# Moving the rounding of weights and one block's sums in the head of a convolution and MLP kernel

## The chip, the cores and the metric

The kernel runs on one core of one Trainium2 chip. The metric is the device time of one execution in microseconds (us); for the kernel before, three runs are given with their median. Engines are named as the profile names them: PE is TensorE (matmuls; PEld its weight loads), DVE is VectorE, ACT is ScalarE, POOL is GpSimd, SP is SyncE, which here only issues transfers. A "q" behind an engine's name is its queue of issued transfers (DMA).

## The reference

The input x = q has 2048 rows of 448 values. Each row is normalized (xn), and the output is the sum of x and two branches:

```python
xn = _layernorm(x, axis=-1)
return x + _A_ref(xn, A_k, A_v, A_shift_k, A_ssm_k, A_ssm_D) + _B_ref(xn, B_w1, B_b1, B_w2)
```

Branch A is a state-space convolution: k goes through a causal convolution of four taps and is multiplied by v (kv); kv is convolved with ssm_k per channel over all 2048 steps by Fourier transforms of length 4096; kv times ssm_D is added; the result is multiplied by xn. Branch B is a two-layer perceptron: h = xn w1 + b1 (1792 columns), act = h tanh(softplus(h)) (Mish), and act w2 (448 columns).

## The kernel before

**The perceptron.** The rows are cut into 8 chunks of 256 (CH), the 1792 hidden columns into 7 pairs of 128-column blocks (NP). One step takes one chunk and one pair: g1_mm (line 474) multiplies xn by w1, mish (line 497) applies bias and Mish on ACT, g2_mm (line 509) multiplies by w2 two steps later (G2_LAG). To keep precision each operand is a high part, rounded to the fp32r type, and a low part, the rest: XH and XL of xn, w1h and w1l, w2h and w2l, ach and acl of the activation. The high part is a copy on ACT, the low part a subtraction on DVE (split, line 79; w1_hi and w1_lo, lines 348 and 351). Each product is three matmuls: high by high, high by low, low by high. In the first chunk g1_mm takes them pair by pair as high weights by XH, high by XL, low weights by XH, and then the remainder of 64 rows (the fourth block of w1h, whose upper half holds its own low part, line 354), first for one block of 128 columns, then for the other; the very first pair has an order of its own (line 490). Its two blocks have a PSUM tile each, those of later pairs share one.

**The convolution** runs between the perceptron's steps: Fourier transforms written as matmuls in three stages. Of the first stage, the head holds one block of ssm_k: f1_mm (line 124) multiplies it by the constant f1 into two PSUM tiles e and o; f1_fold (line 134) copies o to SBUF on ACT and has DVE write the sum and the difference of e and o (lines 138 and 140); f1_out (line 143) stores them to DRAM. The PSUM pool of these blocks holds two tiles (line 52), so the next block's f1_mm waits until both sums are done.

**What sets the order.** The program is scheduled by hand (line 565). Every step has two slots: an even one, in which g1_mm is issued, and an odd one with mish and g2_mm. The lists plan (function at, line 97) and plan2 (function after, line 100) hold what is issued before and after the body of a slot; each engine works through its instructions in the order of issue and waits by semaphores. Before slot 0 comes the head, lines 643 to 700. There SP loads the first chunk of q, the first piece of w1 in two halves, one block of ssm_k (H_HEAD), the second and third pieces of w1 and the first of w2, in that order; ACT issues the loads of the identity (needed by the transposes of xn) and of f1; POOL issues that of the bias b1t (line 666). Then come the statistics of the two row blocks (DVE), the reciprocal standard deviations (POOL, power, line 398), normalization, transposes on PE, and XH and XL. Before the change the block of the head is folded behind slot 3 (line 699); w1's second piece is rounded in slot 0, its third in slot 2, its fourth in slot 4 (line 598); w2's first piece behind slot 3 (line 600). Raw weights pass through a pool of four buffers (kr, line 112): w1's fourth, w2's second, w1's fifth, w2's third and w1's sixth piece each wait for a buffer, and so for the low part made from what it held.

The tile idr has 256 columns: the identity stands in the first 128, and from chunk 5 on the whole tile is overwritten by rows of mean and deviation (nt_row, line 427).

Of the kernel before, what the change touches and what calls it, by code (L numbers as in the profile page):

```python
# [7 lines left out]
F32 = mybir.dt.float32  # L8
# [6 lines left out]
S, D, F = 2048, 448, 1792  # L15
NJ = 16
NF = F // 128
# [6 lines left out]
G2_LAG = 2  # L24
H_HEAD = 1
# [11 lines left out]


@with_exitstack
def tile_kernel(ctx: ExitStack, tc, q, qT, k, v, sk, hT, sD, w10, w1, b1, w2, c_f1, c_id, c_g, c_gi, c_i2, out):  # L40
    nc = tc.nc
    V = nc.vector

    def pool(name, bufs=1, stack=ctx, **kw):
        return stack.enter_context(tc.tile_pool(name=name, bufs=bufs, **kw))

    cp = pool("consts")
# [11 lines left out]
    E = dp.tile([NJ * 4, 64, D], F32, name="E")  # L59
    MR = {c: dp.tile([2, CH], F32, name="MR") for c in range(NT, NCHUNK)}  # L60

    f1 = cp.tile([128, 64], F32, name="f1")
    idr = cp.tile([128, CH], F32, name="idr")
    ident = idr[:, 0:128]
    mhalf = cp.tile([128, 2], F32, name="mhalf")
    b1t = cp.tile([128, NF], F32, name="b1t")
    mv = cp.tile([128, NJ, 2], F32, name="mv")
# [11 lines left out]
    def split(h, l, raw):  # L79
        nc.scalar.copy(h, raw)  # L80
        V.tensor_sub(l, raw, h)  # L81
# [7 lines left out]
    def dv(n=1):  # L89
        for _ in range(n):  # L90
            if drip:
                drip.pop(0)()


    plan, plan2 = {}, {}

    def at(slot, fn, *args):
        plan.setdefault(int(slot), []).append((fn, args))

    def after(slot, fn, *args):  # L100
        plan2.setdefault(int(slot), []).append((fn, args))
# [10 lines left out]
    def kr():  # L112
        return sp1.tile([128, 4, CH], F32, name="kr", bufs=4)
# [17 lines left out]
                    nc.tensor.matmul(ps[h][64 * jj:64 * jj + 64, b, :D], f1[rg:rg + 32], x[rg:rg + 32, jj],  # L131
                                     start=True, stop=True, tile_position=(rg, 64 * jj))

    def f1_fold(g, key):
        ST[key, g] = st = sp1.tile([128, 2, 2, D], F32, name="st", bufs=2)
        e, o = (p[:, :, :D] for p in PS.pop((key, g)))
        nc.scalar.copy(st[:, 1], o)  # L137
        V.tensor_add(st[:, 0], e, st[:, 1])  # L138
        dv()
        V.tensor_sub(st[:, 1], e, st[:, 1])  # L140
        dv()

    def f1_out(dst, g, key, eng=nc.scalar):
        st = ST.pop((key, g))
# [200 lines left out]
    def w1_raw(p, a, b):  # L345
        return RW["1", p][:, :, a:b] if p else RW["1", 0][:, a // 128]

    def w1_hi(p, a=0, b=256):
        nc.scalar.copy(w1h[:, :, 256 * p + a:256 * p + b], w1_raw(p, a, b))

    def w1_lo(p, a=0, b=256):
        fs, rw = slice(256 * p + a, 256 * p + b), w1_raw(p, a, b)
        V.tensor_sub(w1l[:, :, fs], rw[:, 0:3], w1h[:, 0:3, fs])  # L353
        V.tensor_sub(w1h[64:128, 3, fs], rw[64:128, 3], w1h[64:128, 3, fs])
# [5 lines left out]
    def w2_load(p):  # L360
        RW["2", p] = rw = xt() if p > 4 else kr().rearrange("p a b -> p (a b)")[:, :2 * D].rearrange("p (a b) -> p a b", a=2)
        nc.sync.dma_start(rw, w2[:, 2 * p:2 * p + 2])
# [18 lines left out]
    def ln_parts(c):  # L381
        st = mp.tile([128, 2, 6], F32, name="bst", bufs=2)
        ve = mp.tile([128, 2], F32, name="ve", bufs=2)
        if c < NT:
            XN[c] = xn = xn_tile().rearrange("p a b -> p (a b)").rearrange("p (j d) -> p j d", j=2)
        eng = nc.gpsimd if 0 < c < NCHUNK - 1 else V

        def stats(jj):
            V.bn_stats(st[:, jj], Q[c][:, jj])

        def aggr(jj):
            V.bn_aggr(mv[:, 2 * c + jj], st[:, jj])

        def eps(a, b):
            V.tensor_scalar(ve[:, a:b], mv[:, 2 * c + a:2 * c + b, 1], EPS, None, op0=ALU.add)  # L395

        def power(a, b):
            nc.gpsimd.tensor_tensor(rs(c)[:, a:b], ve[:, a:b], mhalf[:, a:b], op=ALU.pow)  # L398

        def norm(jj):  # L400
            j = 2 * c + jj
            eng.tensor_scalar(xn[:, jj, :D], Q[c][:, jj], mv[:, j, 0:1], rs(c)[:, jj:jj + 1],  # L402
                              op0=ALU.subtract, op1=ALU.mult)

        def tail(a, b, copy=eng.tensor_copy):
            copy(xn[:, a:b, D:], xn[:, a:b, D - 64:D])

        return stats, aggr, eps, power, norm, tail, ve
# [88 lines left out]
    def mish(i):  # L497
        p = pairs[i][1]
        ps = P1.pop(i)
        a = mp.tile([128, 2, CH], F32, name="a", bufs=2)  # L500
        for n in range(2):
            nc.scalar.activation(a[:, n], ps[n], AF.Mish, bias=b1t[:, 2 * p + n:2 * p + n + 1])  # L502
        ah = mp.tile([128, 2, CH], F32R, name="ach", bufs=3)
        al = mp.tile([128, 2, CH], F32R, name="acl", bufs=3)
        split(ah, al, a)
        dv()
        AHL[i] = ah, al
# [60 lines left out]
    for g, t in H_AT.items():  # L568
        if g != H_HEAD:
            at(t - 5 if t > 7 else t - 3, h_load, g)  # L570
        if g == 0:
            after(t - 2, lambda: V.tensor_add(HT[0][0:1, 0], HT[0][0:1, 0], SD.pop()))
        at(t, f1_mm, HT, g, "h")
        if t in POOL_H:
            after(t, taps_pool, *POOL_H[t])
        after(t, f1_fold, g, "h")
        at(t + (2 if t < 12 else 3), f1_out, Dh, g, "h", nc.gpsimd if t < 12 else nc.scalar)
# [4 lines left out]
    for g, t in enumerate(KV_AT):  # L582
        d = t - (KV_AT[g - 1] if g else t - 6)
        at(t - d - (3 if g > 1 else 2), k_load, g)
        at(t - d - 1, v_load, g)
        for u in range(4):
            after(t - (2 if g else 1) - d + d * u / 4, taps, g, u)
        at(t, f1_mm, KV, g, "kv")
        if g + 1 < NO:
            after(t, taps_pool, g + 1, 2)  # L590
        after(t, f1_fold, g, "kv")
        at(t + (3 if g < NO - 1 else 2), f1_out, Dkv, g, "kv")

    for p in range(NP):
        if p >= 3:
            at(max(2 * p - 5, 0), w1_load, p)
        if p >= 1:
            at(2 * p - 2, w1_split, p)
        p and at(2 * p + (1 if p < 5 else 0), w2_load, p)
        after(2 * (p + G2_LAG) - 1, w2_split, p)  # L600

    for o in range(NO):
        s, d = OCT_AT[0] + OCT_AT[1] * o, OCT_AT[1]
        h = s - 1 if o else H0_AT
# [50 lines left out]
    nc.gpsimd.tensor_tensor(ve1, one, mhalf, op=ALU.pow)  # L655
    ln_load(0)
    RW["1", 0] = kr().rearrange("p a b -> p (a b)").rearrange("p (n a b) -> p n a b", n=2, a=4)
    nc.scalar.dma_start(ident, c_id)
    nc.scalar.dma_start(f1, c_f1)
    nc.sync.dma_start(RW["1", 0][:, 0], w10[:, 0])  # L660
    h_load(H_HEAD)
    nc.sync.dma_start(RW["1", 0][:, 1], w10[:, 1])
    w1_load(1)
    w1_load(2)
    w2_load(0)
    nc.gpsimd.dma_start(b1t, b1)
    stats, aggr, eps, power, norm, tail, ve = ln_parts(0)
    for jj in range(2):
        stats(jj)
# [26 lines left out]
    x_split(0, 0, ps[0], 1)  # L696
    x_split(0, 1, ps[1], 1)
    w1_lo(0, 128, 256)
    plan2.setdefault(3, []).append((f1_fold, (H_HEAD, "h")))
    plan.setdefault(5, []).insert(0, (f1_out, (Dh, H_HEAD, "h", nc.gpsimd)))  # L700
    for s in range(nslots):
        j = s // 2 - G2_LAG - 1
# [16 lines left out]
def _constants():  # L719
    import numpy as np  # L720

    w = lambda e: np.exp(-2j * np.pi * (np.asarray(e) % 8192) / 8192.0)

    n1 = np.arange(64)
    k1 = np.arange(64)
    W = w(32 * n1[:, None] * (4 * k1[None, :] - 1))

    W = W.reshape(32, 2, 64).transpose(1, 0, 2).reshape(64, 64)
    Wo = W.reshape(64, 8, 2, 4).transpose(0, 1, 3, 2)
    f1 = np.stack([Wo.real, Wo.imag], axis=4).reshape(64, 128)  # L730
    f1 = np.concatenate([f1, f1])

    i2 = np.stack([W.real.T, W.imag.T])[:, :32].reshape(64, 2, 32) / 2048
    i2 = np.concatenate([i2, i2])
    n2 = np.arange(32)[:, None] // 2 + 16 * (np.arange(32)[:, None] % 2)
    k2 = np.arange(32)[None, :]
    G = np.zeros((2, 2, 32, 8, 4, 2, 32))
    GI = np.zeros((4, 32, 8, 2, 2, 2, 16, 2))
    for kk in range(64):
        o, r, t = kk // 8, kk // 4 % 2, kk % 4  # L740
        g = w(n2 * (4 * kk - 1) + 256 * n2 * k2)
        G[r, 0, :, o, t, 0], G[r, 1, :, o, t, 0] = g.real, -g.imag
        G[r, 0, :, o, t, 1], G[r, 1, :, o, t, 1] = g.imag, g.real

        gt = g.T.reshape(32, 16, 2).transpose(0, 2, 1)
        GI[t, :, o, r, 0, ..., 0], GI[t, :, o, r, 1, ..., 0] = gt.real, gt.imag
        GI[t, :, o, r, 0, ..., 1], GI[t, :, o, r, 1, ..., 1] = -gt.imag, gt.real
    c = lambda a: np.ascontiguousarray(a, dtype=np.float32)
    return dict(c_f1=c(f1[:, :64]), c_id=c(np.eye(128)), c_g=c(G.reshape(128, 8, 4, 2, 32)), c_gi=c(GI.reshape(128, 8, 2, 2, 64)),
                c_i2=c(i2))  # L750
# [30 lines left out]
```

## Time and profile before

| | |
|---|---|
| median of 3 runs | 365.65 us (365.17 to 366.61) |
| the profiled execution | 365.54 us |
| its span, first to last instruction | 363.8 us |
| TensorE clock granted | 1.00 of full speed |
| DVE, ACT, POOL busy | 74%, 46%, 20% of the span |
| DMA | 81.69 MB, 225 GB/s over the span |

Times of the trace count from the span's start. A row of the timeline gives start, duration, engine, line of the kernel, operation, output <- inputs by the program's names, shapes and count; in square brackets the time that the engine was idle before it, and what ended that. Consecutive like instructions are one row.

### The profile page before, as it was taken

The numbers are of one execution on the slowest core, as the hardware profiler recorded it, in microseconds if no ns is written. First come the engines' busy times: TensorE is split into PE (matmuls) and PEld (weight loads), VectorE is DVE, ScalarE is ACT, GpSimd is POOL, SyncE is SP. The second block draws the span as 40 slices with busy tenths as digits, with TensorE's granted clock in tenths as the row PEclk, the third lists the DMA queues.
The fourth block names the chain that finished last, engine by engine and source line by source line (L and its number), as shares of the span: only waits on it lengthen the run. The fifth ranks groups of instructions, "written<-read, shape, count | busy, mean of one in ns | idle before, by whom it ended". The sixth has DMA issues, their size and how long they took to land.

```text
span 363.8 us, 7470 instructions
## 1 busy us (share of the span) xinstructions
PE 357.3 (98%) x3108; PEld 289.8 (80%) x3108; DVE 267.6 (74%) x367; ACT 166.5 (46%) x279; POOL 73.8 (20%) x66
## 2 busy tenths in 40 slices
PE   7999999999999999999999999999999999999995
PEld 2888888888888989988967666666666889889885
DVE  5799758999998988797427755767665734997741
ACT  4876642344333433343255555547645534225450
POOL 3027002941028223604000020000010005112020
PEclk9999999999999999999999999999999999999999
DMA  7999978758586438524876799998897485969655
GB/s 241 352 271 370 392 311 232 224 153 270 152 268 195 94 121 269 145 70 116 235 263 212 261 239 226 290 255 223 282 288 172 89 252 198 406 258 280 109 68 134
DMA packets 32628, 81.69 MB, mean 225 GB/s; under 512 B 3154, under 2 KB 19155, under 8 KB 32595
## 3 DMA queue, kind: packets, MB, share of 16 engines
q1 hardware_dynamic: 21266, 47.16, 38.9%
q10 hardware_dynamic: 8384, 19.37, 21.7%
q0 software_dynamic: 2944, 14.70, 13.9%
q8 instruction: 24, 0.39, 0.4%
q14 instruction: 10, 0.07, 0.1%
HBM read 52.77 MB, written 28.45 MB: 223 GB/s over the span
## 4 chain that ended last, share of the span: by engine, by line
PE 54%; DVE 2%; ACT 1%; ACTq 1%; issue 0%
PE pg L494 20%; PE pg L519 7%; PE pc L214 7%; PE pg L521 7%; PE pg L520 7%; PE pc L257 4%; PE pc L314 2%; ACTq L268 1%; DVE x L178 1%; PE pc L131 1%; DVE x L181 0%; ACT qe L265 0%; ACT a L502 0%; ACT hs L225 0%; DVE qt L526 0%
## 5 line engine op out<-in xcount | busy, mean ns | idle before, releaser
L502 ACT ACTIVATE a<-pg,b1t 128x256 f32<-128x256 f32 x112 | 47.2, 472 | 109.1 <-PE pg L494 95.8
L494 PE MATMUL pg<-XH,w1h 128*128 128x256 f32 x448 | 90.5, 284 | 0.2 <-DVE XL L457 0.2
L494 PEld LDWEIGHTS pg<-XH,w1h 128*128 128x128 f32 x448 | 69.6, 188 | 18.4 <-issue 15.8
L519 PE MATMUL pg<-w2h,ach 128*128 128x448 f32 x224 | 83.2, 371 | 0.0
L520 PE MATMUL pg<-w2l,ach 128*128 128x448 f32 x224 | 81.4, 363 | 0.4 <-DVE w2l L81 0.4
L521 PE MATMUL pg<-w2h,acl 128*128 128x448 f32 x224 | 81.4, 363 | 0.0
L81 DVE TENSOR_TENSOR acl<-a,ach 128x512 fp32r<-128x512 f32 x56 | 38.7, 691 | 57.5 <-ACT ach L80 57.4
L494 PE MATMUL pg<-XL,w1h 128*128 128x256 f32 x448 | 71.3, 277 | 0.0
L494 PEld LDWEIGHTS pg<-XL,w1h 128*128 128x128 f32 x448 | 60.2, 188 | 0.0
L494 PE MATMUL pg<-XH,w1l 128*128 128x256 f32 x336 | 56.9, 278 | 0.0
L519 PEld LDWEIGHTS pg<-w2h,ach 128*128 128x128 f32 x224 | 42.0, 187 | 14.4 <-issue 12.2
L494 PEld LDWEIGHTS pg<-XH,w1l 128*128 128x128 f32 x336 | 46.8, 188 | 0.2 <-DVE w1l L353 0.2
L520 PEld LDWEIGHTS pg<-w2l,ach 128*128 128x128 f32 x224 | 42.1, 188 | 3.3 <-DVE w2l L81 0.9
L521 PEld LDWEIGHTS pg<-w2h,acl 128*128 128x128 f32 x224 | 42.1, 188 | 2.5
L80 ACT CAST ach<-a 128x512 fp32r<-128x512 f32 x56 | 34.7, 620 | 1.8
L161 POOL TENSOR_TENSOR x<-kr,skb 128x896 f32<-128x896 f32 x8 | 17.0, 2129 | 74.5 <-DVE x L160 53.1
L178 DVE TENSOR_TENSOR x<-x 128x896 f32<-128x896 f32 x24 | 26.3, 1097 | 2.7 <-POOL x L161 2.2
L398 POOL TENSOR_TENSOR mv<-ve,mhalf 128x2 f32<-128x2 f32 x3 | 3.8, 1250 | 97.9 <-DVE ve L395 97.9
L402 POOL TENSOR_SCALAR xn<-qt,mv,rstd 128x448 f32<-128x448 f32 x8 | 21.8, 2721 | 0.4
L137 ACT COPY st<-pc 128x896 f32<-128x896 f32 x16 | 14.5, 906 | 14.0 <-PE pc L131 12.6
L138 DVE TENSOR_TENSOR st<-pc,st 128x896 f32<-128x896 f32 x16 | 17.4, 1088 | 4.0 <-ACT st L137 3.7
L265 ACT COPY qe<-pc 128x896 f32<-128x896 f32 x16 | 13.8, 912 | 12.0 <-PE pc L257 12.0
(84 smaller groups left out, 402.6 us busy)
## 6 DMA issues: line engine op xcount, KB each, us to landing
Dkv<-st ACTq DMA_DIRECT2D x16, 448.0 KB, 6.2
ah<-Dh SPq DMA_DIRECT2D x8, 896.0 KB, 7.4
av<-Dkv SPq DMA_DIRECT2D x8, 896.0 KB, 6.8
E<-qe ACTq DMA_DIRECT2D x16, 448.0 KB, 5.5
e<-E POOLq DMA_DIRECT2D x8, 896.0 KB, 8.5
kr<-in_k_dram SPq DMA_DIRECT2D x10, 448.0 KB, 6.5
Dh<-st ACTq DMA_DIRECT2D x10, 448.0 KB, 5.6
x<-in_hT_dram SPq DMA_DIRECT2D x8, 448.0 KB, 6.3
```

The source lines that it names most:

```text
L80: nc.scalar.copy(h, raw)
L81: V.tensor_sub(l, raw, h)
L138: V.tensor_add(st[:, 0], e, st[:, 1])
L161: nc.gpsimd.tensor_mul(o, KR[g - u // 2], skb[:, u:u + 1].to_broadcast([128, 2, D]))
L178: V.tensor_add(KV[g], KV[g], o)
L214: nc.tensor.matmul(p[32 * t:32 * t + 32, r, :D], g[rs, t, c], a[rs, t], start=True, stop=True, tile_position=(64 * r, 32 * t))
L402: eng.tensor_scalar(xn[:, jj, :D], Q[c][:, jj], mv[:, j, 0:1], rs(c)[:, jj:jj + 1], op0=ALU.subtract, op1=ALU.mult)
L494: nc.tensor.matmul(ps[n], l, r, start=all(m[0] != n for m in seq[:n_]), stop=all(m[0] != n for m in seq[n_ + 1:]))
L502: nc.scalar.activation(a[:, n], ps[n], AF.Mish, bias=b1t[:, 2 * p + n:2 * p + n + 1])
L519: nc.tensor.matmul(ps, ah[:, n, cs], w2h[:, f], start=f == 0, stop=False)
L520: nc.tensor.matmul(ps, ah[:, n, cs], w2l[:, f], start=False, stop=False)
L521: nc.tensor.matmul(ps, al[:, n, cs], w2h[:, f], start=False, stop=f == NF - 1)
```

## The change

Three edits, all in the head:

- The identity, f1 and the bias come in one transfer, issued by ACT, into the first 206 columns of idr; f1 is a part of that tile, and POOL copies the bias out of it into b1t. The separate loads of f1 (ACT) and of the bias (POOL) go, and so do their inputs.
- w1's third piece is rounded inside the first step's mish: ACT's copy stands between the two Mish activations, DVE's low part ahead of the activation's own low part. w2's first piece is rounded in slot 2, before g1_mm, no longer behind slot 3.
- The fold of the head's block is split. ACT's copy and DVE's sum are issued at the end of the head, behind the low part of w1's first piece; the difference in slot 2, behind the low part of w2's first piece.

```diff
-    f1 = cp.tile([128, 64], F32, name="f1")
     idr = cp.tile([128, CH], F32, name="idr")
-    ident = idr[:, 0:128]
+    ident, f1 = idr[:, 0:128], idr[:, 128:192]
...
-    def f1_fold(g, key):
+    def f1_fold(g, key, parts=False):
         ST[key, g] = st = sp1.tile([128, 2, 2, D], F32, name="st", bufs=2)
         e, o = (p[:, :, :D] for p in PS.pop((key, g)))
         nc.scalar.copy(st[:, 1], o)
-        V.tensor_add(st[:, 0], e, st[:, 1])
-        dv()
-        V.tensor_sub(st[:, 1], e, st[:, 1])
-        dv()
+
+        def part(n):
+            f = V.tensor_sub if n else V.tensor_add
+            f(st[:, n], e, st[:, 1])
+            dv()
+
+        if not parts:
+            part(0)
+            part(1)
+        return part
...
         for n in range(2):
             nc.scalar.activation(a[:, n], ps[n], AF.Mish, bias=b1t[:, 2 * p + n:2 * p + n + 1])
+            if i == n == 0:
+                w1_hi(2)
+        if i == 0:
+            w1_lo(2)
...
-        if p >= 1:
+        if p == 1 or p > 2:
             at(2 * p - 2, w1_split, p)
         p and at(2 * p + (1 if p < 5 else 0), w2_load, p)
-        after(2 * (p + G2_LAG) - 1, w2_split, p)
+        at(2, w2_split, p) if p == 0 else after(2 * (p + G2_LAG) - 1, w2_split, p)
...
-    nc.scalar.dma_start(ident, c_id)
-    nc.scalar.dma_start(f1, c_f1)
+    nc.scalar.dma_start(idr[:, 0:192 + NF], c_fib)
+    nc.gpsimd.tensor_copy(b1t, idr[:, 192:192 + NF])
...
-    nc.gpsimd.dma_start(b1t, b1)
...
     w1_lo(0, 128, 256)
-    plan2.setdefault(3, []).append((f1_fold, (H_HEAD, "h")))
+    part = f1_fold(H_HEAD, "h", True)
+    part(0)
+    at(2, part, 1)
...
+    const = _constants()
+    const["c_fib"] = np.concatenate([const.pop("c_id"), const.pop("c_f1"), a["B_b1"].reshape(NF, 128).T], axis=1)
```

More of the change, by code (lines that the diff above doesn't have):

```diff
@@ L39, in tile_kernel @@
 @with_exitstack
-def tile_kernel(ctx: ExitStack, tc, q, qT, k, v, sk, hT, sD, w10, w1, b1, w2, c_f1, c_id, c_g, c_gi, c_i2, out):
+def tile_kernel(ctx: ExitStack, tc, q, qT, k, v, sk, hT, sD, w10, w1, w2, c_fib, c_g, c_gi, c_i2, out):
     nc = tc.nc
@@ L766 @@
         v=lay(a["A_v"][0]), sk=a["A_shift_k"].T, hT=lay(a["A_ssm_k"].T), sD=a["A_ssm_D"][None],
-        w10=w1[:, :, 0].reshape(4, 128, 2, 128).transpose(1, 2, 0, 3), w1=w1.transpose(2, 1, 0, 3), b1=a["B_b1"].reshape(NF, 128).T,
-        w2=a["B_w2"].reshape(NF, 128, D).transpose(1, 0, 2), **_constants())
+        w10=w1[:, :, 0].reshape(4, 128, 2, 128).transpose(1, 2, 0, 3), w1=w1.transpose(2, 1, 0, 3),
+        w2=a["B_w2"].reshape(NF, 128, D).transpose(1, 0, 2), **const)
     nc = bacc.Bacc("TRN2", target_bir_lowering=False, num_devices=1)
```

## The prediction

> **What bounds the kernel now.** I read the page first, then the timeline of TensorE (PE) over the first 32 us and, beside it, those of VectorE (DVE), ScalarE (ACT) and GpSimd (POOL).
>
> ```profile
> span 363.8 us, 7470 instructions
> ...
> PE 357.3 (98%) x3108; PEld 289.8 (80%) x3108; DVE 267.6 (74%) x367; ACT 166.5 (46%) x279; POOL 73.8 (20%) x66
> ```
>
> PE works 357.3 of 363.8 us, so only its gaps can be won. The change touches the head, and there PE shows three gaps (start, duration, instructions, idle time before them and what ended it):
>
> ```profile
> 8.18 1.01 PE L131 MATMUL pc<-x,f 32*64 32x448 f32 x16 [0.44 <-DMA x<-in_hT_dram]
> ...
> 12.40 0.50 PE L494 MATMUL pg<-XH,w1l 128*128 128x256 f32 x3
> 12.74 0.28 PE L494 MATMUL pg<-XH,w1h 128*128 128x256 f32 x1
> 12.86 0.28 PE L494 MATMUL pg<-XL,w1h 128*128 128x256 f32 x1
> ...
> 14.56 0.50 PE L494 MATMUL pg<-XL,w1h 128*128 128x256 f32 x3
> 15.05 0.62 PE L494 MATMUL pg<-XH,w1l 128*128 128x256 f32 x3
> 15.51 0.38 PE L494 MATMUL pg<-XH,w1h 128*128 128x256 f32 x1
> 15.72 0.28 PE L494 MATMUL pg<-XL,w1h 128*128 128x256 f32 x1
> ...
> 17.14 0.37 PE L519 MATMUL pg<-w2h,ach 128*128 128x448 f32 x1
> 17.93 0.47 PE L520 MATMUL pg<-w2l,ach 128*128 128x448 f32 x1 [0.43 <-DVE w2l L81]
> 18.24 0.37 PE L521 MATMUL pg<-w2h,acl 128*128 128x448 f32 x1
> 18.45 0.37 PE L519 MATMUL pg<-w2h,ach 128*128 128x448 f32 x1
> ```
>
> Matmuls overlap, so a stall is read from starts, not from idle time. Undisturbed, three first-product matmuls take 0.34 us (12.40 to 12.74), one 0.12 (12.74 to 12.86), and one second-product matmul 0.21 (18.24 to 18.45). Against that:
> - 8.18: the f1 block waits 0.44 us for its data.
> - 15.05: 14.56 to 15.05 is 0.49 (0.15 too long), to 15.51 0.46 (0.12), to 15.72 0.21 (0.09). Together **0.36 us**.
> - 17.93: 17.14 to 17.93 is 0.79 (0.58 too long), to 18.24 0.31 (0.10). Together **0.68 us**.
>
> Who is late there is read from DVE and ACT:
>
> ```profile
> 10.04 0.29 DVE L354 TENSOR_TENSOR w1h<-kr,w1h 64x128 fp32r<-64x128 f32 x1
> 11.14 0.96 DVE L353 TENSOR_TENSOR w1l<-kr,w1h 128x768 fp32r<-128x768 f32 x1 [0.81 <-ACT w1h L349]
> ...
> 14.04 0.96 DVE L353 TENSOR_TENSOR w1l<-kr,w1h 128x768 fp32r<-128x768 f32 x1 [0.26 <-ACT w1h L349]
> 15.03 0.42 DVE L354 TENSOR_TENSOR w1h<-kr,w1h 64x256 fp32r<-64x256 f32 x1
> 15.94 0.69 DVE L81 TENSOR_TENSOR acl<-a,ach 128x512 fp32r<-128x512 f32 x1 [0.49 <-ACT ach L80]
> 16.79 1.09 DVE L81 TENSOR_TENSOR w2l<-kr,w2h 128x896 fp32r<-128x896 f32 x1
> 17.80 1.08 DVE L138 TENSOR_TENSOR st<-pc,st 128x896 f32<-128x896 f32 x1
> ...
> 28.61 1.08 DVE L81 TENSOR_TENSOR w2l<-kr,w2h 128x896 fp32r<-128x896 f32 x1
> ```
>
> ```profile
> 7.77 0.65 ACT L459 CAST XH<-pg 128x256 fp32r<-128x256 f32 x2 [0.43 <-PE pg L447]
> 8.80 0.62 ACT L349 CAST w1h<-kr 128x512 fp32r<-128x512 f32 x1 [0.38 <-DMA kr<-in_w_dram]
> 10.06 1.05 ACT L349 CAST w1h<-kr 128x1024 fp32r<-128x1024 f32 x1 [0.64 <-DMA kr<-in_w_dram]
> ...
> 12.96 1.05 ACT L349 CAST w1h<-kr 128x1024 fp32r<-128x1024 f32 x1
> ...
> 15.82 0.94 ACT L80 CAST w2h<-kr 128x896 fp32r<-128x896 f32 x1
> 16.66 0.90 ACT L137 COPY st<-pc 128x896 f32<-128x896 f32 x1
> ...
> 29.12 1.05 ACT L349 CAST w1h<-kr 128x1024 fp32r<-128x1024 f32 x1 [2.68 <-DMA kr<-in_w_dram]
> ```
>
> The low part of w1's third piece ends at 14.04 + 0.96 = 15.00, and PE goes on at 15.05; its partial row ends at 15.45, and PE's next step is 15.51. The low part of w2's first piece ends at 16.79 + 1.09 = 17.88, and PE goes on at 17.93. Both stalls are late DVE work, and DVE had idled before it: 0.81 us before 11.14, 0.26 before 14.04, 0.49 before 15.94.
>
> **The change, part by part.**
>
> *The block's sum and difference.* The st copy (0.90) moves on ACT behind the cast at 8.80, the sum (1.08) on DVE behind 10.04. ACT: 8.80 + 0.62 = 9.42, copy to 10.32, w1's second cast (1.05) to 11.37. PE needs it at 11.72, where the second pair begins (two groups of 0.34 before 12.40), so this is covered by 0.35. DVE: 10.04 + 0.29 = 10.33, sum to 11.4, low parts of the second piece 0.96 to 12.4 and 0.42 to 12.8. PE wants these at 12.40 and 12.74: about 0.1 late. Before, they ended at 12.10 and 12.55. So the sum fills the 0.81 of idle time and overshoots by 0.27; most of the overshoot is old slack. If ACT's cast comes no sooner, the cost is 0.1 to 0.3.
>
> *w1's third piece.* Its cast (1.05) goes between the first pair's two Mish activations: 11.9 to 12.9, instead of 12.96. It holds the second Mish and the block's cast back by about 0.6, which only g2's first product at 17 needs. DVE takes the low parts at 12.9, to 13.9 and 14.3, against needs of 14.9 and 15.25. The 0.36 us stall goes; next behind it is nothing within 0.9 us.
>
> *w2's first piece.* Its cast (0.94) runs on ACT at about 13.7 to 14.6, before the second pair's Mish. DVE goes on from 14.3: the first pair's acl (0.69) to 15.0, w2l (1.09) to 16.1, needed at 17.0. The 0.68 us stall goes with 0.9 us to spare. Then the difference (1.09) to 17.2, the second pair's acl (0.69) to 17.9, w1's fourth piece (0.96 + 0.42) to 19.2. The second f1 block reuses the two PSUM tiles and would now start at 20.34 - 1.04 = 19.3; they are free at 17.2.
>
> *One transfer for three.* ACT issues one DMA instead of two, POOL none; a POOL copy of 128x14 is added, ahead of the two rstd powers.
>
> ```profile
> 4.74 0.58 POOL L398 TENSOR_TENSOR rstd<-ve,mhalf 128x1 f32<-128x1 f32 x1 [2.35 <-DVE ve L395]
> 5.66 0.75 POOL L398 TENSOR_TENSOR rstd<-ve,mhalf 128x1 f32<-128x1 f32 x1 [0.34 <-DVE ve L395]
> ...
> 28.83 0.96 POOL L406 COPY xn<-xn 128x64 f32<-128x64 f32 x1
> ...
> 31.70 0.24 POOL L406 COPY xn<-xn 128x64 f32<-128x64 f32 x1
> ```
>
> ```profile
> skb<-in_sk_dram SPq DMA_DIRECT2D x1, 896.0 KB, 10.4
> ```
>
> ```profile
> f<-in_c_f_dram ACTq DMA_DIRECT2D x1, 32.0 KB, 3.3
> b1t<-in_b_dram POOLq DMA_DIRECT2D x1, 7.0 KB, 4.9
> ```
>
> The copy waits for the transfer, and behind it on POOL stand the two powers, then DVE's normalization, the transposes and XH. No landing of the identity's transfer is recorded. Issued at 0.9, it lands at 4.2 with f1's 3.3 us and at 5.8 with the bias's 4.9; the copy takes 0.24 to 0.96. So it ends between 4.4 and 6.8. The first power starts at 4.74; the second, on which XH hangs, at 5.66, so the copy may end at 5.08 (5.66 - 0.58) at no cost. Beyond that XH has its own cover: it is ready at 7.77 + 0.65 = 8.42, while PE is in the f1 block until 9.1. Thus free up to 5.7, at worst 1.1 us. I take **0**: f1's row is the nearest, same queue and issuer.
>
> Which of the copy's two prices holds can be weighed with the Trainium skill, page "SBUF — State Buffer", section "Who interferes with whom": a VectorE instruction with two SBUF inputs and a GpSimd instruction that reads SBUF exclude each other, and the later waits for the earlier's end. The trace agrees: the copy of 0.96 stands beside the two-input w2l of 28.61 to 29.69, that of 0.24 does not. In the head DVE runs one-input statistics then, so by that page it would be 0.24, and the sum is the same either way.
>
> On the other side the bias's 7 KB leave the DMA engines just as the f1 block's data (x) travels. x may land 0 to 0.44 us sooner. I take 0.2, and with it the cast at 8.80. But the second pair then waits for DVE as worked out above, and 0.1 to 0.2 of it is given back. The two together: **0** (bounds 0.3 lost, 0.2 won).
>
> *Later.* What is earlier in the head must also arrive earlier. The nearest place is PE at 35.68:
>
> ```profile
> 35.31 0.45 PE L519 MATMUL pg<-w2h,ach 128*128 128x448 f32 x1
> 35.68 0.47 PE L520 MATMUL pg<-w2l,ach 128*128 128x448 f32 x1
> ```
>
> ```profile
> 21.39 0.33 SPq L343 DMA_DIRECT2D kr<-in_w_dram x1
> ```
>
> ```profile
> kr<-in_w_dram SPq DMA_DIRECT2D x1, 512.0 KB, 7.7
> ```
>
> There 0.37 stands for 0.2: a stall of some 0.17 (0.27 with its ramp) behind DVE, which runs without a break from w1's sixth piece on; ACT waited 2.68 us for that piece and took it at 29.12. Its landing, 21.39 + 7.7 = 29.1, thus reaches PE at 35.68, 6.6 us later. Its issue waits for DVE's fourth piece, now at 19.2 and not 21.3. With the same 7.7 us it lands at 27.0, and the stall goes (0.27 won). With no gain in landing, PE arriving 1.04 sooner gives all of it back there. It needs to land by about 28.1 to keep the stall as it is. The first block's store (POOL, 20.32 until now) starts at 17.2 and takes its share of the engines, so I do not count the full 2.1 us: I take **0**.
>
> Sum: -0.36 - 0.68 = -1.04 us. From the profiled execution's 365.54 (span 363.8 and 1.7 around it) this gives 364.5. That execution lies 0.11 under the median of 365.65; I stay at **364.5**.
>
> **Rivals.**
> 1. *Given back at 35.7.* w1's sixth piece lands at about 29.1 as before. For it: ACT's wait of 2.68 us shows the transfers, not the issuers, as late there. Against: the issue comes 2.1 us sooner. Time: 364.5 + 1.0 = 365.5.
> 2. *Slower.* The block's store, 3.1 us earlier, goes ahead of w1's sixth piece. From a landing after 29.1 each us costs one. If that piece needs the 10.4 us of the longest transfer of this stretch, it lands at 19.2 + 10.4 = 29.6, 1.5 after 28.1: 366.0. Against: the store must be through by then, as it starts sooner too.
> 3. *The bias's copy holds rstd.* Decides from a copy that ends after 5.7; at 6.8 it costs 1.1: 365.6.
> 4. *It doesn't do what it says*: w1's third or w2's first piece is no sooner, because its own transfer is late. Against: both casts at 12.96 and 15.82 started without a wait for a DMA; one stall at most remains: 365.1.
>
> **How the numbers follow.** The forecast 0.60, given back 0.16, slower 0.10, copy 0.07, not sooner 0.07. Single runs of before reach from 0.48 under to 0.96 over their median. The forecast's own bounds are 364.5 - 0.27 - 0.2 = 364.0 and 364.8; under the lower one I put the 0.48 of scatter, about 363.6, and above, the slower rival's 366.0 with a tenth, 366.1. About 0.5% (1.8 us) is what a measurement of this kernel can tell from no change. Faster by more than that means under 363.8: every stall of the head and the one at 35.7 add up to 0.44 + 1.04 + 0.27 = 1.75, so only scatter reaches it, 0.05. Slower by more needs over 367.5, a landing 3 us late in the slower case: 0.05. Within: 0.90.
>
> **What would show it.** In the profile after: no idle time of PE before L520 near 17; DVE without its 0.81 us pause; w1l's third low part ending near 13.9 and w2l's first near 16.1; PE's second f1 block at about 19.3; SP's issue of w1's sixth piece near 19.2 and ACT's cast of it before 28.1. Wrong would be: POOL's first power after 5.1, PE's L520 near 34.6 waiting longer than 0.2, or a new wait at the second pair over 0.3.

## The result, and the profile after

The changed kernel takes 364.73 us in the median (364.21 to 367.27, 22 runs), the kernel before 365.69 (365.17 to 366.61, 22 runs beside it). The ratio is 0.9975 (95% interval 0.9965 to 0.9984): 0.9 us faster, clear of noise but inside half a per cent. Two executions of other kernels below ran at a lower granted clock (0.92 and 0.75) and took 377.61 and 445.05 us; the ratios leave them out. The profiled execution took 364.74 us, its span is 363.0. Its page:

```profile
span 363.0 us, 7466 instructions
...
PE 357.0 (98%) x3108; PEld 290.0 (80%) x3108; DVE 268.0 (74%) x367; ACT 166.6 (46%) x279; POOL 71.4 (20%) x66
```

With the same 3108 matmuls PE's busy time fell by 0.3 us (357.3 to 357.0) and its idle time by 0.5 (6.5 to 6.0 us). Both are stalls that went: where matmuls overlap, a stall also shows as longer rows. In the timeline of PE the f1 block starts at 7.73 and not 8.18, the third pair runs through from 14.31, L529 (the L520 of before: lines have moved) no longer waits, and the second f1 block starts at 19.30:

```profile
7.73 1.01 PE L130 MATMUL pc<-x,idr 32*64 32x448 f32 x16
8.67 0.62 PE L499 MATMUL pg<-XH,w1h 128*128 128x256 f32 x3
...
11.17 0.28 PE L499 MATMUL pg<-XL,w1h 128*128 128x256 f32 x1
11.48 0.62 PE L499 MATMUL pg<-XH,w1h 128*128 128x256 f32 x3
11.93 0.52 PE L499 MATMUL pg<-XL,w1h 128*128 128x256 f32 x3
12.29 0.58 PE L499 MATMUL pg<-XH,w1l 128*128 128x256 f32 x3
12.71 0.38 PE L499 MATMUL pg<-XH,w1h 128*128 128x256 f32 x1
12.93 0.28 PE L499 MATMUL pg<-XL,w1h 128*128 128x256 f32 x1
...
14.31 0.50 PE L499 MATMUL pg<-XH,w1h 128*128 128x256 f32 x3
14.65 0.50 PE L499 MATMUL pg<-XL,w1h 128*128 128x256 f32 x3
14.99 0.50 PE L499 MATMUL pg<-XH,w1l 128*128 128x256 f32 x3
...
16.80 0.36 PE L528 MATMUL pg<-w2h,ach 128*128 128x448 f32 x1
17.00 0.36 PE L529 MATMUL pg<-w2l,ach 128*128 128x448 f32 x1
...
19.30 1.01 PE L130 MATMUL pc<-x,idr 32*64 32x448 f32 x16
```

DVE, in the same stretch, has no pause left from the first low parts to w1's fourth piece at 17.34:

```profile
9.92 0.29 DVE L359 TENSOR_TENSOR w1h<-kr,w1h 64x128 fp32r<-64x128 f32 x1
10.24 1.09 DVE L140 TENSOR_TENSOR st<-pc,st 128x896 f32<-128x896 f32 x1
11.25 0.95 DVE L358 TENSOR_TENSOR w1l<-kr,w1h 128x768 fp32r<-128x768 f32 x1
12.23 0.42 DVE L359 TENSOR_TENSOR w1h<-kr,w1h 64x256 fp32r<-64x256 f32 x1
12.68 0.96 DVE L358 TENSOR_TENSOR w1l<-kr,w1h 128x768 fp32r<-128x768 f32 x1
...
14.73 1.08 DVE L80 TENSOR_TENSOR w2l<-kr,w2h 128x896 fp32r<-128x896 f32 x1
...
17.34 0.95 DVE L358 TENSOR_TENSOR w1l<-kr,w1h 128x768 fp32r<-128x768 f32 x1
```

The difference of starts of the same matmul in both traces is the lead of the new kernel. It is 0.45 us at the first f1 block (8.18 - 7.73) and lost again by the second pair's 12.93 (-0.07, against 12.86). Of this 0.52, 0.31 goes where the second pair begins: 11.17 to 11.48 is 0.31 for 0.11, and the next step 0.45 for 0.34. There PE's weight load (PEld) waits for the first Mish activation on ACT. The pool of these PSUM tiles (ps_g1, line 50) has two, the first pair holds both, and the second pair reuses the one that this Mish reads:

```profile
11.47 0.41 PEld L499 LDWEIGHTS pg<-XH,w1h 128*128 128x128 f32 x3 [0.22 <-ACT a L507]
```

```profile
10.00 1.05 ACT L354 CAST w1h<-kr 128x1024 fp32r<-128x1024 f32 x1
10.95 0.48 ACT L507 ACTIVATE a<-pg,b1t 128x256 f32<-128x256 f32 x1
```

That Mish ends at 11.43, behind the cast of w1's second piece. The piece landed at 9.95, only 0.09 us sooner than before (10.04), while the f1 block's data x came 0.36 sooner (7.69 against 8.05); so ACT's copy in front held the cast back by 0.05 us at most. The other 0.2 us go at the low parts, behind the sum on DVE.

Past the third pair and w2's first piece it is 1.04, and still 1.04 at the second f1 block (20.34 - 19.30). At 35 it grows, at 188 it shrinks. First PE at w2's fourth piece, where 34.27 to 34.55 is now 0.28 and before was 0.37, so that the lead is 1.13 there, and 1.23 one matmul on (35.98 before, 34.76 now):

```profile
34.27 0.45 PE L528 MATMUL pg<-w2h,ach 128*128 128x448 f32 x1
34.55 0.37 PE L529 MATMUL pg<-w2l,ach 128*128 128x448 f32 x1
```

and PE at the first product of the convolution's second stage (after, and behind it before):

```profile
187.09 0.63 PE L499 MATMUL pg<-XL,w1h 128*128 128x256 f32 x4
188.03 1.36 PE L219 MATMUL pc<-av,g 64*32 64x448 f32 x24 [0.30 <-DMA av<-Dkv]
```

```profile
188.34 0.63 PE L494 MATMUL pg<-XL,w1h 128*128 128x256 f32 x4
188.90 1.36 PE L214 MATMUL pc<-av,g 64*32 64x448 f32 x24
```

PE reaches this point 1.2 us sooner than before and waits for av; of its lead 0.87 is left (188.90 - 188.03), and stays to the end. The lists of transfers show why: av took longer from its issue to landing, 6.5 us in the first row (after, issued at 181.35), 5.2 in the second (before, issued at 182.58). It landed at 187.9 and 187.8, as late in both.

```profile
av<-Dkv SPq DMA_DIRECT2D x1, 896.0 KB, 6.5
```

```profile
av<-Dkv SPq DMA_DIRECT2D x1, 896.0 KB, 5.2
```

### The profile page after: what moved, and what is told of

It is laid out like the page before. It is cut to its first block, busy times and chain, and to the rows that moved or that the text cites. A ratio compares the mean times of both kernels' runs of the same rounds, so it can differ in the third digit from the quotient of the medians.

```text
span 363.0 us, 7466 instructions
## 1 busy us (share of the span) xinstructions
PE 357.0 (98%) x3108; PEld 290.0 (80%) x3108; DVE 268.0 (74%) x367; ACT 166.6 (46%) x279; POOL 71.4 (20%) x66
## 4 chain that ended last, share of the span: by engine, by line
PE 49%; DMA 4%; DVE 2%; ACT 1%; ACTq 1%; issue 0%
PE pg L499 18%; PE pg L528 7%; PE pc L219 6%; PE pg L530 6%; PE pg L529 6%; PE pc L262 4%; PE pc L319 2%; DMA av<-Dkv 2%; DMA Dkv<-st 2%; ACTq L273 1%; DVE st L140 1%; DVE x L183 1%; ACT a L507 0%; DVE qt L535 0%; DVE x L186 0%
## 5 line engine op out<-in xcount | busy, mean ns | idle before, releaser
L529 PE MATMUL pg<-w2l,ach 128*128 128x448 f32 x224 | 81.2, 362 | 0.0
L529 PEld LDWEIGHTS pg<-w2l,ach 128*128 128x128 f32 x224 | 42.1, 188 | 2.4
L140 DVE TENSOR_TENSOR st<-pc,st 128x896 f32<-128x896 f32 x32 | 34.8, 1089 | 4.5 <-ACT st L136 3.8
L407 POOL TENSOR_SCALAR xn<-qt,mv,rstd 128x448 f32<-128x448 f32 x8 | 20.5, 2566 | 0.4
```

The lines of the kernel that those rows point to most:

```text
L140: f(st[:, n], e, st[:, 1])
L529: nc.tensor.matmul(ps, ah[:, n, cs], w2l[:, f], start=False, stop=False)
```

## The experiments

The landing of the first f1 block's data differs from execution to execution, whatever the kernel. So the head is compared by two stretches that begin with that block: from the first f1 block to the third pair's start, and from the first f1 block to the second one. They are not free of every landing: w1's second piece landed 2.22 us after the block's start in the first profile of the whole change, and 1.24 to 2.10 after it in the others. All times in us; "ratio" is to the kernel before, run beside it.

| kernel | f1 to third pair | f1 to f1 | median | ratio (95%) |
|---|---|---|---|---|
| before | 6.04 | 12.16 | 365.69 | |
| the whole change | 6.58 | 11.57 | 364.73 | 0.9975 (0.9965 to 0.9984) |
| one transfer alone | 6.07 | 12.20 | 365.74 | 0.9995 (0.9986 to 1.0004) |
| w1's third piece alone | 6.05 | 12.18 | 365.65 | 0.9995 (0.9984 to 1.0005) |
| w2's first piece alone | 6.04 | 11.47 | 365.05 | 0.9980 (0.9968 to 0.9993) |
| both pieces | 6.14 | 11.13 | 364.86 | 0.9966 (0.9954 to 0.9979) |
| transfer and both pieces | 6.05 | 11.05 | 364.67 | 0.9962 (0.9949 to 0.9974) |
| both pieces and fold | 6.52 | 11.51 | 364.68 | 0.9961 (0.9948 to 0.9975) |
| whole, sum in slot 2 | 6.13 | 11.12 | 364.62 | 0.9966 (0.9952 to 0.9980) |
| whole, again | 6.59 | 11.58 | 364.39 | 0.9959 (0.9947 to 0.9970) |
| whole, POOL held in the head | 6.45 | 11.55 | 365.75 | 0.9993 (0.9982 to 1.0004) |
| transfer and both pieces, a store by ACT | 6.31 | 11.41 | 364.80 | 0.9973 (0.9963 to 0.9983) |
| the same, the store behind a cast | 6.23 | 11.33 | 364.04 | 0.9946 (0.9932 to 0.9959) |

The last two rows have no sum in the head, and yet took 0.2 to 0.3 us more than "transfer and both pieces". Between the first f1 block and the third pair, three first-product matmuls start 0.35 to 0.36 us apart there for much of the way, and not 0.34, and in the upper one PE also loses about 0.1 at the first Mish. Why they do is open. So without the sum in front the stretch took 6.04 to 6.31, with it 6.45 to 6.59.

**One transfer alone**, in the kernel before:

```diff
-    nc.scalar.dma_start(ident, c_id)
-    nc.scalar.dma_start(f1, c_f1)
+    nc.scalar.dma_start(idr[:, 0:192 + NF], c_fib)
+    nc.gpsimd.tensor_copy(b1t, idr[:, 192:192 + NF])
...
-    nc.gpsimd.dma_start(b1t, b1)
```

> Only the one transfer for identity, f1 and bias; rounding and fold as before. Theory (what comes sooner in the head is taken back by ACT and DVE): the first f1 block starts near 7.75 instead of 8.18, but the second pair of matmuls then waits for the first Mish activation and w1's low parts, so the second f1 block starts 0.1 to 0.3 us sooner than 20.34, PE still stalls near 17.9 before w2's low part, and the time is 0.0 to 0.4 us under before. Rival (the transfer is worth its 0.45 us): second f1 block near 19.9, time 0.45 under before or more.

The f1 block started at 7.92, the second one at 20.12, 0.22 us sooner, and w2's low part was still waited for; the time is that of before. The lead was not lost at the second pair (6.07 against 6.04), as the theory had it there, but at w2's sixth low part at 47 (below). Over 13 profiles x landed at 8.05, 7.16, 7.92, 8.12 and 8.26 us with three transfers and at 7.69, 7.88, 7.10, 7.32, 8.22, 7.66, 7.67 and 7.85 with one. The medians are 8.05 and 7.68; the ranges overlap.

**Both pieces sooner**, with transfers and fold as before:

```diff
             nc.scalar.activation(a[:, n], ps[n], AF.Mish, bias=b1t[:, 2 * p + n:2 * p + n + 1])
+            if i == n == 0:
+                w1_hi(2)
+        if i == 0:
+            w1_lo(2)
...
-        after(2 * (p + G2_LAG) - 1, w2_split, p)
+        at(2, w2_split, p) if p == 0 else after(2 * (p + G2_LAG) - 1, w2_split, p)
```

> Only w1's third and w2's first piece rounded sooner; transfers and fold as before. Theory (the two stalls of 0.36 and 0.68 us are late DVE work, and nothing else is needed to remove them): second f1 block at 19.3, all of the 1.04 us, the second pair's 12.40 unchanged; w1's sixth piece is issued near 20.5, lands near 28, and PE stalls 0.0 to 0.3 at 34.6; time 0.8 to 1.1 under before. Rival (the fold has to leave its place too): the sums end after 19.3 and hold the second f1 block, which starts at 19.6 or later; time 0.3 to 0.6 under before.

From f1 to f1 1.03 us went (12.16 - 11.13). The second f1 block was not held by the sums. The gain is that of the whole change without its other two parts.

**One transfer and both pieces**, the fold behind slot 3:

> One transfer and sooner rounding, the fold as before behind slot 3. Theory: the first f1 block near 7.75; without the copy and the sum in the way the second pair loses only what the first Mish takes back (about 0.2 us), so 0.1 to 0.3 us of the transfer's 0.45 are left: second f1 block at 19.0 to 19.2; time 0.9 to 1.3 under before, no less than the whole change. Rival (the fold's new place is part of the gain): second f1 block after 19.3 and the time above the whole change's.

1.11 us went from f1 to f1, and nothing was lost at the second pair. The time is no more than the whole change's.

**Both pieces and the fold**, three transfers:

> Sooner rounding and the fold's new place, with the three transfers as before. Theory (in the whole change the copy and the sum in front of w1's second piece cost what the transfer won): the first f1 block at 8.18, w1's second low parts end near 12.4 and 12.8, the second pair loses 0.1 to 0.3, and the second f1 block starts at 19.4 to 19.6; time 0.6 to 0.9 under before. Rival (the overshoot costs nothing): second f1 block at 19.3.

The second pair lost 0.48 us (6.52 - 6.04) although the f1 block started late here, at 8.47 (behind the transposes; x had landed at 7.92): the loss belongs to the order, not to x. It is larger than expected. Its second f1 block started at 19.99, not at 19.4 to 19.6: 0.3 of that is the first one's late start.

**The sum out of the head**, ACT's copy still in it:

```diff
     part = f1_fold(H_HEAD, "h", True)
-    part(0)
+    at(2, part, 0)
     at(2, part, 1)
```

> The whole change, but of the fold only ACT's copy stays at the end of the head; DVE's sum goes to slot 2, ahead of the difference. In the two runs with the sum in front (the changed kernel, and rounding with the fold but without the one transfer) the third pair began 6.58 and 6.52 us after the first f1 block, in those without it 6.04 to 6.14. Theory (both engines share this loss: the copy holds the first Mish, on whose PSUM tile the second pair waits, and the sum holds w1's second low parts): 6.2 to 6.4 here. Rival (DVE's sum alone): 6.0 to 6.15. Rival (ACT's copy alone): 6.5 or more. The time cannot tell them apart.

6.13: without DVE's sum in front nearly all of the loss is gone, with ACT's copy still there. The first Mish took nothing here: w1's second piece had landed at 9.53, the copy held its cast until 9.65, and the Mish ended at 11.09, before the second pair's 11.26. In the first profile of the whole change the Mish was late because the piece landed at 9.95; the copy held its cast for 0.05 at most. No profile here shows that the copy cost more than that 0.05 us.

**The whole change again**:

> The whole change again, on the same chip as the other three, for a profile of another execution. Theory (the loss of the copy and the sum ahead of w1's second piece belongs to the order, the landing of the f1 block's data to the execution): 11.4 to 11.7 from the first to the second f1 block, wherever the first one starts; time 0.7 to 1.1 under before. Rival (the loss was that execution's): under 11.3.

6.59 and 11.58, with the f1 block at 7.90 this time. The loss shows on PE at the second pair:

```profile
11.81 0.51 PE L499 MATMUL pg<-XL,w1h 128*128 128x256 f32 x3
12.42 0.62 PE L499 MATMUL pg<-XH,w1l 128*128 128x256 f32 x3
12.88 0.39 PE L499 MATMUL pg<-XH,w1h 128*128 128x256 f32 x1
13.10 0.29 PE L499 MATMUL pg<-XL,w1h 128*128 128x256 f32 x1
```

and on DVE, where sum and low parts stand one behind the other:

```profile
10.41 1.09 DVE L140 TENSOR_TENSOR st<-pc,st 128x896 f32<-128x896 f32 x1
11.42 0.95 DVE L358 TENSOR_TENSOR w1l<-kr,w1h 128x768 fp32r<-128x768 f32 x1
12.40 0.42 DVE L359 TENSOR_TENSOR w1h<-kr,w1h 64x256 fp32r<-64x256 f32 x1
```

The low part ends at 12.37 and PE goes on at 12.42, 0.27 late (11.81 + 0.34 = 12.15); the row ends at 12.82 and PE goes on at 12.88, another 0.12; the next takes 0.22 for 0.12. It is the pattern of the third pair before, and sums to 0.49. The first profile of the same kernel has the same loss, in part from another cause: 0.31 at the first Mish and 0.2 at the low parts. The two do not add up there: without the Mish's wait PE would have come to the low part at about 11.95 (7.73 + 12.40 - 8.18) and waited for it until 12.20 all the same.

**w1's third piece alone**, the first half of the edit for both pieces:

> The kernel before with one edit: w1's third piece is rounded between the first two Mish activations; w2's first piece stays behind slot 3. Measured from the first to the second f1 block (12.16 us before, 11.13 with both pieces sooner), so that the landing of the block's data does not count. Theory (the two stalls stand one behind the other, and w2's low part waits for ACT's earlier work, not for DVE's): the 0.36 us at the third pair go, PE comes sooner to w2's first piece and waits 0.9 to 1.1 there; 12.0 to 12.2, time as before. Rival (the two terms add): 11.8, time 0.36 under before.

12.18: nothing. PE comes to w2's first product sooner, and waits longer there:

```profile
16.69 0.28 PE L494 MATMUL pg<-XL,w1h 128*128 128x256 f32 x1
16.90 0.47 PE L523 MATMUL pg<-w2h,ach 128*128 128x448 f32 x1
18.03 0.48 PE L524 MATMUL pg<-w2l,ach 128*128 128x448 f32 x1 [0.66 <-DVE w2l L81]
```

16.90 to 18.03 is 1.13 for 0.2: 0.93 us late, nearly the whole of 0.36 + 0.68.

**w2's first piece alone**, in slot 2 behind w1's third:

```diff
-        after(2 * (p + G2_LAG) - 1, w2_split, p)
+        p and after(2 * (p + G2_LAG) - 1, w2_split, p)
+    at(2, w2_split, 0)
```

> The kernel before with one edit: w2's first piece is rounded in slot 2, behind w1's third piece. Theory: the 0.36 us before w1's third low part stay, the 0.68 us before w2's go: 11.4 to 11.6 from the first to the second f1 block, time 0.4 to 0.9 under before. Rival (the low part of w2 now holds the second pair's activation or the sums, and a new wait comes up): 11.8 or more.

11.47, so 0.69 us went, and the third pair's stall is still there (14.77 to 15.27 on PE is 0.50 for 0.34).

**POOL held in the head**, in the whole change:

```diff
     nc.gpsimd.tensor_copy(b1t, idr[:, 192:192 + NF])
+    pad = cp.tile([128, 64], F32, name="pad")
+    for _ in range(8):
+        nc.gpsimd.tensor_copy(pad, idr[:, 0:64])
```

> The whole change with eight more POOL copies of 128x64, of a part of the identity into a scratch tile, behind the copy of the bias and ahead of the two rstd powers: POOL is free at about 5.9 and not at 4.1. Theory (the copy is free until about 5.1, beyond that the normalization comes later one for one, and XH has some 0.2 us of cover behind the f1 block): the second power starts near 6.5 instead of 5.69, the first pair near 9.3 instead of 8.67, the second f1 block 0.2 to 0.7 us later than 19.3, as the second pair has less to give back; time 0.2 to 0.6 over the changed kernel. Rival (the f1 block covers it wholly): first pair at 8.7 to 8.9, time as the changed kernel.

The copies took longer than expected, so POOL was free at 6.38. Its timeline, and PE's:

```profile
3.92 0.19 POOL L668 COPY b1t<-idr 128x14 f32<-128x14 f32 x1 [2.23 <-DMA idr<-in_c_fib_dram]
4.05 2.33 POOL L671 COPY pad<-idr 128x64 f32<-128x64 f32 x8
6.34 1.14 POOL L403 TENSOR_TENSOR rstd<-ve,mhalf 128x1 f32<-128x1 f32 x2
```

```profile
8.35 0.66 PE L452 MATMUL pg<-idr,xn 128*128 128x128 f32 x4
8.93 1.01 PE L130 MATMUL pc<-x,idr 32*64 32x448 f32 x16
9.87 0.38 PE L499 MATMUL pg<-XH,w1h 128*128 128x256 f32 x1
```

The first pair started at 9.87 and not 8.67, the second f1 block at 20.48 and not 19.30: 1.2 us. In the changed kernel the second power starts at 5.69 and the first takes 0.55, so POOL is free of cost up to 5.14; from there it is one for one (6.38 - 5.14 = 1.24). The time was 365.75 (ratio 0.9993, 0.9982 to 1.0004), no gain over the kernel before that could be told from noise. The theory's one for one holds; its 0.2 us of cover, and the rival with it, are refuted: the f1 block gives no cover, as on PE it stands behind the transposes and comes later with them.

**Later stretches.** Where is the lead lost after the head? Three edits of "one transfer and both pieces", whose profile shows PE waiting at w2's sixth low part, 46.06. Its cause was traced back: ACT's copy of a later block waited until 41.25 for a buffer whose store POOL issued only at 31.39, behind the normalization of the second chunk:

```profile
28.53 2.56 POOL L401 TENSOR_SCALAR xn<-qt,mv,rstd 128x448 f32<-128x448 f32 x1
...
31.39 1.31 POOL L145 DMA_DIRECT2D Dh<-st  x2
```

The store by ACT's queue:

```diff
-        at(t + (2 if t < 12 else 3), f1_out, Dh, g, "h", nc.gpsimd if t < 12 else nc.scalar)
+        at(t + (2 if t < 12 else 3), f1_out, Dh, g, "h", nc.gpsimd if t == 9 else nc.scalar)
```

> One transfer and sooner rounding, and the store of the second block of ssm_k goes by ACT's queue in slot 8 and no longer by POOL's, where it stands behind the normalization of the second chunk (issued at 31.4 in the run of rounding and one transfer, though its sums were done by 26.5). Theory (the wait of PE at 46 to 47 for w2's sixth low part, in three of the five profiles so far, comes from this store: ACT's copy of a later block waits for its buffer until 41.2): issued by 27, landed by 37, ACT's copy near 38, and no wait of PE at 46; time 0 to 0.4 under rounding and one transfer. Rival (the transfer engines are full from 30 to 48, so the order alone does nothing): it lands after 40 all the same, or another transfer is late in its place, and the time is the same.

The copy ran at 39.33 and PE did not wait at 46. But ACT now issued the store ahead of its cast of w1's sixth piece:

```profile
26.89 1.31 ACTq L145 DMA_DIRECT2D Dh<-st  x2
28.24 1.05 ACT L348 CAST w1h<-kr 128x1024 fp32r<-128x1024 f32 x1 [3.03 <-DVE acl L80]
```

so that the cast, whose piece had landed at 25.47, began at 28.24, and PE waited 0.3 us near 35. Time 364.80 (0.9973, 0.9963 to 0.9983), no better.

The same store behind that cast:

```diff
-        at(t + (2 if t < 12 else 3), f1_out, Dh, g, "h", nc.gpsimd if t < 12 else nc.scalar)
+        (after if t < 9 else at)(t + (2 if t < 12 else 3), f1_out, Dh, g, "h", nc.gpsimd if t == 9 else nc.scalar)
```

> One transfer and sooner rounding, and the second block's store goes by ACT's queue, this time behind the cast of w1's sixth piece (in the earlier run it stood ahead of it and held that cast until 28.2). Theory (the waits of PE at 35.7 and at 46 both follow from what stands in a queue ahead: this order frees both): cast of w1's sixth piece as soon as it lands, no wait of PE at 35.7 nor at 46, the lead of 20 us kept to 60 us within 0.1; time 0 to 0.5 under that of rounding and one transfer. Rival (the transfer engines are full from 30 to 48 and give the gain back at another place): a wait of 0.2 or more between 35 and 60 all the same, or at the second stage from 188 on, time no better.

The cast runs as soon as its piece has landed, the copy at 38.71, and PE has neither wait:

```profile
26.72 1.05 ACT L348 CAST w1h<-kr 128x1024 fp32r<-128x1024 f32 x1 [1.58 <-DMA kr<-in_w_dram]
26.82 1.31 ACTq L145 DMA_DIRECT2D Dh<-st  x2
```

The lead was 1.30 at 18, 1.49 from 36 to 226, and 1.82 at the end. The last 0.33 are not the store's: the kernel before loses them in its own profile from 226 on (0.27 at one wait of PE there), and the profiles of "one transfer alone", "w2's first piece alone" and "whole, again" win them too. Time 364.04, ratio 0.9946 (0.9932 to 0.9959), the lowest of all and faster than before. The intervals overlap with those of the whole change run beside it (0.9959, 0.9947 to 0.9970) and of the kernel that it starts from (0.9962, 0.9949 to 0.9974); only the interval of the whole change's first 22 runs (0.9975, down to 0.9965) lies apart. So the profile shows the two waits gone, and the times do not show for certain that this is worth anything.

The last kv block's store in two queues:

```diff
-            eng.dma_start(dst.rearrange(
+            (nc.gpsimd if jj and (key, g) == ("kv", NO - 1) else eng).dma_start(dst.rearrange(
```

> One transfer and sooner rounding, and the second half of the last kv block's store goes by POOL's queue and not behind the first half on ACT's. Theory (where the lead is lost at 188.9, the second stage waits for the round trip of that store through DRAM, and its two halves run one behind the other at half rate): the second half lands 1 us or more sooner than 5.7 us after its issue, the load of av behind it with it, and PE does not wait before L214's av; the lead of about 1.4 us at 180 lasts to the end in this execution. Rival (the transfer engines are full there): both halves land as late as before, and nothing changes.

Time 364.84 (0.9974, 0.9965 to 0.9984), no gain over the kernel that it starts from. Its one profile is of the execution of 445.05 us, which cannot be set beside the others; whether the halves landed sooner stays open.

## Why the prediction was right

*The two stalls.* Right in place, size and sum: from the third pair's start to the second f1 block it was 6.12 us (14.22 to 20.34) and is 4.99 (14.31 to 19.30), so 1.13 went; 1.04 was summed. DVE's low parts ended at 13.64 (w1's third piece) and 15.81 (w2's first), against 13.9 and 16.1 forecast. What the sum did not say is that the 0.36 is worth nothing alone. The two stand one behind the other, and w2's low part sets when PE goes on; w1's third piece counts only once that is removed. The run with w1's third piece alone shows it. So the fourth rival was priced too low: with w2's first piece late, not 0.4 us but nothing would have been left (12.18 against 12.16).

*The block's sum in front.* The direction was right, the size wrong, and one of the prediction's own signs of being wrong did appear: a new wait at the second pair over 0.3. "0.1 to 0.3" was worked out from the overshoot of DVE; in four profiles with the sum in front the stretch to the third pair takes 0.41 to 0.55 more than before (6.45 to 6.59 against 6.04). Two steps failed. The prediction compared two ends with two needs, and left out that PE is late for the low part, then again for the row, and ramps up after each: in the second profile 0.27 late at the low part became 0.49. And it asked when PE needs the second cast (11.72, "covered by 0.35"), but not when the first Mish behind that cast frees the second pair's PSUM tile: with its own 11.37 and a Mish of 0.47 that is about 11.75 to 11.84, so there was no cover. In the first profile, with PE 0.45 us ahead, this cost 0.31. Undoing the fold alone costs nothing: the kernel with the other two parts and the old fold is as fast within its interval. This part of the change bought nothing that these runs show.

*One transfer.* "0" for transfer and sum together was nearly right in this profile (0.45 won, 0.54 lost by the third pair), but made of two larger numbers than 0.2 and 0.2; that is luck. Part of what x won would not have been kept in this execution with the old fold either (an estimate: the first Mish, behind w1's second piece, would have ended at 11.38 or later, and PE wanted its tile at about 11.27). The transfer alone shows no gain in time.

*The bias's copy.* It ended at 4.14 and cost nothing, near the lower bound of 4.4:

```profile
3.95 0.19 POOL L668 COPY b1t<-idr 128x14 f32<-128x14 f32 x1 [2.26 <-DMA idr<-in_c_fib_dram]
4.76 0.55 POOL L403 TENSOR_TENSOR rstd<-ve,mhalf 128x1 f32<-128x1 f32 x1 [0.62 <-DVE ve L400]
5.69 0.75 POOL L403 TENSOR_TENSOR rstd<-ve,mhalf 128x1 f32<-128x1 f32 x1 [0.38 <-DVE ve L400]
```

The statistics that DVE runs beside it read one SBUF input each; that such a pair, outside VectorE's two-port modes, does not exclude each other, as the Trainium skill has it (page "SBUF — State Buffer", section "Who interferes with whom"), agrees with the 0.19. One row was misread: beside the copy of 0.24 at 31.70 before, DVE's acl, which has two SBUF inputs, does start, at 31.79, so that row is no case without such a neighbour. The profile after has a clear pair: the copy at 26.85 took 0.96 and ended 0.10 after w2l (26.62 to 27.71), the one at 30.52 took 0.24 beside a sum with one input in PSUM. The free time up to 5.1 was right; the further cover up to 5.7 was not there. The failed step is "XH has its own cover": it took the f1 block's place on PE as fixed, though the block is queued behind the transposes. At the upper bound of 6.8 the price would have been 1.7 us and not 1.1.

*Later.* w1's sixth piece was issued at 18.80 (19.2 was forecast), landed 7.9 us later at 26.7 (27.0), and the wait at 35 went: 0.19 us won, where 0 was taken and 0.27 was the bound. The first rival, the lead given back to a late transfer, did occur, but elsewhere: 0.36 at av, 153 us further on, a place that the prediction did not look at. In the second profile of the whole change that wait is absent, and the lead at the end is 1.41. Five profiles of other kernels lose 0.2 to 1.3 us at 47. So the end was right partly by luck, because gains and losses that were not counted offset each other: -1.13 + 0.09 - 0.19 + 0.36 = -0.87 at the last matmul; the spans differ by 0.8.

## What to carry to other kernels

A stall is worth its length only if nothing stands behind it; where two follow each other on one engine, the chance is in the second, and edits are to be tried one by one as well as together. Work that is put into an engine's pause must end before the work behind it is needed, and 0.27 us of lateness cost 0.49 here, as the waiting engine was stopped twice. Ask of each instruction not only who needs its result, but also what stands behind it on its engine and which buffer that frees. What is won in the head is kept only as far as the stores and loads behind it are sooner too: look for the queue in which an early transfer stands behind unrelated work.

## What was not expected of the hardware

- The same transfer of 448 KB, third in its queue, landed between 7.10 and 8.26 us in 13 profiles. In eight of them the f1 block started 0.04 to 0.14 us behind it; in the other five it had landed 0.37 to 0.85 before, and the block stood behind the transposes.
- Eight POOL copies of 128x64 took 2.33 us, 0.29 each; one of 128x14 took 0.19.
- The load of av, 896 KB, took 5.2 us in one execution and 6.5 in another for nearly the same landing. In which of several places a lead is lost differs from execution to execution of the same kernel.
